# Attention scores in float32, two heads side by side on TensorE's rows, with one PSUM bank for h

## The chip, the cores and the metric

The kernel runs on one core of one Trainium2 chip. The metric is the time of the core in microseconds (us). The core has five engines with queues of their own: TensorE (PE; its weight loads are listed as PEld), VectorE (DVE), ScalarE (ACT), GpSimd (POOL), and SyncE (SP), which issues DMAs. PSUM has eight banks that hold the products until another engine reads them.

## The reference

Windowed attention over 8 batches, 8 heads, 576 positions of 64 features, then a two-layer network on its output. All data are float32.

```python
scores = scale * np.matmul(q, k.transpose(0, 1, 3, 2))
slopes = 2.0 ** (-8.0 * (np.arange(H, dtype=np.float32) + 1) / H)
mask = (rel >= 0) & (rel < 128)                    # rel = query - key
scores = np.where(mask, scores + slopes * -np.abs(rel), -1e9)
attn = softmax(scores); x = attn @ v               # x: 4608 x 512
h = x @ w_in                                       # 512 -> 2048
g = h * erf(softplus(h))
out = g @ w_out                                    # 2048 -> 512
```

## The kernel before

Heads go in pairs: 32 pairs (8 batches of 4), each with a q and a k array of 128 rows, 64 rows for each of the two heads. A pair has five tiles of 128 queries (`QTILES`, the last overlaps the fourth): tile 0 sees 128 keys, tiles 1 to 3 see 256, tile 4 sees 192. Tiles 0 to 2 are span 0, tiles 3 and 4 span 1. The first eight pairs run span 0 of all eight, then span 1; later pairs run whole.

One tile's way: scores on TensorE into PSUM (line 511, or 497 for the first spans), bias and row minimum on VectorE (522), exponential on ScalarE (532), sums on VectorE (549, 550), scaling on GpSimd (560), transposes on TensorE (578, tile `t`), copies out of PSUM (472 on ScalarE, 474 on VectorE), products with v on TensorE (596, `px`).

The scores are taken in one of two ways. Spans of the first four pairs (`EARLY`) use two float32 products, one for each head, on 64 rows each, in two PSUM buffers; q alone is scaled, by VectorE (line 435). All others split q and k for the float32r type: `kh` is k in float32r (451 on VectorE or 453 on ScalarE), `kl` what is left of it (463, VectorE), and `a` holds q in float32r on one half of the rows (472 or 474) and its residual on the other (466, GpSimd). Then four products of 128 rows fill one bank for both heads. For that k is loaded twice, once for each half of the rows, through one raw buffer each for k and q.

The second part (`Moe`) runs in units: a chunk of 384 tokens by 128 hidden features. A unit takes 12 products into `h` (line 782, PSUM, two buffers), a copy to SBUF (766 on ScalarE or 768 on VectorE), softplus and erf on ScalarE (811, 813), products on VectorE (824, 829), and 9 products into `o` (844). 72 units use the first 6 blocks of the weights and 120 the other 10. Weights are prepared by VectorE, ScalarE and GpSimd (lines 670 to 692), `x` is split by VectorE (759).

The order of all work is fixed when the program is built. `Plan.run` takes every operation with an assumed cost, a due time `at` and its buffers, and places it on its engine when its inputs and buffers are free, the earliest due first. Forty warm-up products (line 383) fill TensorE where nothing else is ready. So other costs or other buffers give another order on every engine.

PSUM's eight banks before: `h` two, `o` three, `s`, `t` and `x` one each.

Of the kernel before, what the change touches and what calls it, by code (L numbers as in the profile page):

```python
# [19 lines left out]
P = 128  # L20
# [13 lines left out]
EARLY = 4  # L34
# [6 lines left out]
PB, XB, OB, TB, TBB = 8, 3, 3, 2, 2  # L41
BT = 0
# [279 lines left out]
def step_time(n):  # L322
    return TE * min(n, NE) + TA * max(0, n - NE)
# [19 lines left out]
class Attention:  # L343


    def __init__(self, tc, plan, ctx, actx, qT, kT, vb, bias, ident, moe):
# [5 lines left out]
        self.raw, self.split, self.pp, self.ptp, self.xsb = (  # L352
            sb(n) for n in ("raw", "split", "pp", "ptp", "xsb")
        )
# [10 lines left out]
        self.seq = 0  # L365
# [20 lines left out]
    def operands(self, i, w=None):  # L386

        nc, op = self.nc, self.plan.op
        sync = nc.sync.dma_start
        b, g = self.order[i]  # L390
        at = step_time(self.step) - LL
        q0, q1 = (0, S) if w is None else SPANS[w][1:3]
        k0 = max(0, q0 - WIN)
        nq, nk = q1 - q0, q1 - k0
        early = self.seq < EARLY
        nm = f"{i}_{w}"
        tags = [("a0", "kh0"), ("a1", "kh1"), ("kl0", "kl1")][self.seq // 2 % 3]
        self.seq += 1
        if early:
            q = Buf(self.split, [P, S], F32, tags[0], 2, "a" + nm)  # L400
            k = Buf(self.split, [P, S], F32, tags[1], 2, "k" + nm)
            op(emit=lambda e: sync(k[:, :nk], self.kT[b, g, :, k0:q1]), w=[k], at=at, **dma(P * nk * 4))
        else:
            q = Buf(self.raw, [P, S], F32, "qr", 1, "qr" + nm)
            k = Buf(self.raw, [P, 2, S], F32, "kr", 1, "kr" + nm)
            src = self.kT[b, g, :, k0:q1].rearrange("(j d) s -> d j s", j=2)

            def both(e):
                for half in range(2):
                    sync(k[half * D : (half + 1) * D, :, :nk], src)  # L410

            op(emit=both, w=[k], at=at, **dma(2 * P * nk * 4, 2, 0.65))
        op(emit=lambda e: sync(q[:, :nq], self.qT[b, g, :, q0:q1]), w=[q], at=at, **dma(P * nq * 4))
        at = step_time(self.step) - LP
        return (*(self.early_parts if early else self.parts)(nm, g, q, k, nq, nk, at), q0, k0)
# [16 lines left out]
    def early_parts(self, nm, g, q, k, nq, nk, at):  # L432
        for j in range(2):
            rows = slice(j * D, (j + 1) * D)
            self.plan.op({"DVE": dve(nq, True)}, lambda e, j=j, rows=rows: self.nc.vector.tensor_scalar(
                q[rows, :nq], q[rows, :nq], 2.0 ** (2 * g + j), None, op0=ALU.mult), r=[q], w=[q], at=at)
        return q, k, None

    def parts(self, nm, g, q, k, nq, nk, at):

        nc, op = self.nc, self.plan.op
        lo, hi = slice(0, D), slice(D, P)
        a = [Buf(self.split, [P, S], F32R, f"a{j}", 2, f"a{nm}_{j}") for j in range(2)]
        kh = [Buf(self.split, [P, S], F32R, f"kh{j}", 2, f"kh{nm}_{j}") for j in range(2)]
        kl = [Buf(self.split, [P, S], F32R, f"kl{j}", 2, f"kl{nm}_{j}") for j in range(2)]

        def scaled(e, out, src, by):
            if e == "DVE":  # L450
                nc.vector.tensor_scalar(out, src, by, None, op0=ALU.mult)
            else:
                nc.scalar.mul(out, src, by)

        either = lambda n: {"DVE": dve(n, True), "Act": act(n)}
        for j in range(2):
            own, other = (lo, hi) if j == 0 else (hi, lo)
            by = 2.0 ** (2 * g + j)
            op(either(nk), lambda e, j=j, by=by: scaled(e, kh[j][:, :nk], k[:, j, :nk], by),
               r=[k], w=[kh[j]], at=at)  # L460
            op(either(nq), lambda e, j=j, own=own: self.copy(e, a[j][own, :nq], q[own, :nq]),
               r=[q], w=[a[j]], at=at)
            op({"DVE": dve(nk)}, lambda e, j=j, by=by: nc.vector.scalar_tensor_tensor(
                kl[j][:, :nk], k[:, j, :nk], by, kh[j][:, :nk], op0=ALU.mult, op1=SUB),
                r=[k, kh[j]], w=[kl[j]], at=at)
            op({"Pool": pool_tt(nq)}, lambda e, j=j, own=own, other=other: nc.gpsimd.tensor_tensor(  # L466
                a[j][other, :nq], q[own, :nq], a[j][own, :nq], SUB), r=[q, a[j]], w=[a[j]], at=at)
        return a, kh, kl

# [6 lines left out]
    def scores(self, i, t, operands, low, total, at):  # L476
# [5 lines left out]
        a, kh, kl, q0, k0 = operands  # L482
        k0 = start - WIN + c0 * 64 - k0
        q0 = start - q0
        src = []
        if kl is None:

            ways = [((self.ps, "s", 1), (self.ps, "t", 1))]
            if i < NPAIR and t < 3:
                ways = [((self.ps, "s", 1), (self.spare[1], "o0", 1)), ((self.spare[0], "h", 2),) * 2]  # L490
            for j, (pool, tag, bufs) in enumerate(ways[self.step % len(ways)]):
                src.append((Buf(pool, [P, 2, 256], F32, tag, bufs, f"s{i}_{t}_{j}"), 0))

            def products(e):
# [473 lines left out]
```

## Time and profile before

| what | value |
|---|---|
| median of 3 runs | 1118.45 us (1116.33 to 1119.25) |
| profiled execution | 1118.25 us |
| its span, first to last instruction | 1116.3 us |
| TensorE busy | 1073.7 us (96%) |
| ScalarE busy | 721.9 us (65%) |
| VectorE busy | 684.9 us (61%) |
| GpSimd busy | 385.7 us (35%) |
| mean granted TensorE clock | 0.983 of 2.4 GHz |

A matmul's time in the profile runs until its result is out, and the next one starts long before that; what a matmul keeps TensorE for is read from start to start. A float32 product stands as two matmuls. Names are the program's, with buffer numbers left out: `s` scores, `p` probabilities, `t` transposes, `st` row minima and sums. "<-" behind an idle time names what ended it.

### The profile page before, as it was taken

How to read it: one execution, taken by the hardware profiler on the slowest of the kernel's cores; microseconds unless marked ns; L12 is line 12 of the kernel's file. 1: busy time of each engine (PE TensorE's matmuls, PEld its weight loads, DVE VectorE, ACT ScalarE, POOL GpSimd, SP SyncE). 2: the span in 40 equal slices, each digit the busy share in tenths (PEclk: the TensorE clock that was granted, in tenths of full speed). 3: DMA queues.
4: the chain of work that ended last, by engine and by line, in shares of the span. 5: the costliest groups of instructions: out<-in, count | busy, mean ns of one | idle time of the engine just before them, and what ended most of it. 6: DMA issues, size and time to landing. Idle time of an engine off the chain costs nothing.

```text
span 1116.3 us, 17069 instructions
## 1 busy us (share of the span) xinstructions
PE 1073.7 (96%) x6000; PEld 976.5 (87%) x6000; DVE 684.9 (61%) x1602; ACT 721.9 (65%) x1436; POOL 385.7 (35%) x464
## 2 busy tenths in 40 slices
PE   9776979999999999999999999999999999999998
PEld 8666968988899999999899998899999999999996
DVE  5878898887888888775867675333433433433332
ACT  6567667878788787776677675355455455455462
POOL 5776887646666566653333231000000000000000
PEclk9797999999999999999999999999999999999999
DMA  6444555444545455422343422202202202202102
GB/s 184 139 132 122 140 152 153 146 132 115 163 118 135 121 143 149 118 89 78 114 132 114 141 69 74 86 13 73 85 19 67 85 19 67 85 13 73 57 19 67
DMA packets 89732, 111.59 MB, mean 100 GB/s; under 512 B 45744, under 2 KB 59696, under 8 KB 89648
## 3 DMA queue, kind: packets, MB, share of 16 engines
q1 hardware_dynamic: 89648, 110.52, 33.5%
q8 instruction: 47, 0.77, 0.3%
q14 instruction: 37, 0.30, 0.1%
HBM read 82.18 MB, written 28.31 MB: 99 GB/s over the span
## 4 chain that ended last, share of the span: by engine, by line
PE 82%; DVE 9%; POOL 3%; DMA 2%; issue 2%; ACT 2%; POOLq 0%; SPq 0%; DVEq 0%; ACTq 0%
PE o L844 32%; PE h L782 31%; PE px L596 7%; PE s L511 5%; PE t L578 5%; POOL p L560 2%; DMA xr<-xd 2%; DVE p L522 1%; PE warm_ps L383 1%; DVE xl L759 1%; POOL wto L686 1%; DVE hs L824 1%; DVE gl L829 1%; PE s L497 1%; ACT p L532 1%
## 5 line engine op out<-in xcount | busy, mean ns | idle before, releaser
L782 PE MATMUL h<-xh,whi 128*128 128x384 f32 x768 | 262.5, 342 | 0.0
L782 PE MATMUL h<-xl,whi 128*128 128x384 f32 x768 | 259.2, 338 | 1.6 <-DVE xl L759 1.6
L782 PE MATMUL h<-xh,wli 128*128 128x384 f32 x768 | 259.7, 338 | 0.0
L560 POOL TENSOR_SCALAR p<-p,st 128x256 f32<-128x256 f32 (+2 forms) x320 | 194.0, 623 | 128.1 <-DVE st L550 108.1
L844 PE MATMUL o<-who,gh 128*128 128x512 f32 x576 | 228.8, 397 | 0.6 <-DVE ot L768 0.6
L844 PE MATMUL o<-who,gl 128*128 128x512 f32 x576 | 227.6, 395 | 1.2 <-DVE gl L829 1.2
L844 PE MATMUL o<-wlo,gh 128*128 128x512 f32 x576 | 227.3, 395 | 1.2 <-POOL wlo L692 0.7
L766 ACT COPY hs<-h 128x384 f32<-128x384 f32 x137 | 65.3, 477 | 215.1 <-PE h L782 214.6
L532 ACT ACTIVATE p<-p,st 128x256 f32<-128x256 f32 (+2 forms) x320 | 149.0, 468 | 24.5 <-DVE st L522 23.6
L782 PEld LDWEIGHTS h<-xl,whi 128*128 128x128 f32 x768 | 145.2, 189 | 8.7 <-DVE xl L759 2.1
L782 PEld LDWEIGHTS h<-xh,whi 128*128 128x128 f32 x768 | 145.3, 189 | 6.9 <-ACT hs L766 0.2
L782 PEld LDWEIGHTS h<-xh,wli 128*128 128x128 f32 x768 | 144.8, 189 | 0.2 <-POOL wli L692 0.2
L844 PEld LDWEIGHTS o<-who,gl 128*128 128x128 f32 x576 | 108.1, 188 | 25.4 <-DVE gl L829 2.1
L522 DVE CUSTOM_DVE_ANT_0 p<-s,bias_sb 128x256 f32<-128x256 f32 (+2 forms) x320 | 109.4, 378 | 33.4 <-PE s L511 21.6
L768 DVE COPY hs<-h 128x384 f32<-128x384 f32 x55 | 30.4, 554 | 160.8 <-PE h L782 160.8
L844 PEld LDWEIGHTS o<-wlo,gh 128*128 128x128 f32 x576 | 108.5, 188 | 17.9 <-POOL wlo L692 2.2
L844 PEld LDWEIGHTS o<-who,gh 128*128 128x128 f32 x576 | 108.6, 188 | 16.6 <-DVE ot L768 1.5
L824 DVE TENSOR_TENSOR hs<-s,hs 128x768 f32<-128x768 f32 x96 | 95.2, 1016 | 23.4 <-ACT s L813 23.4
L829 DVE TENSOR_TENSOR gl<-hs,gh 128x768 fp32r<-128x768 f32 x96 | 94.6, 989 | 15.5 <-ACT gh L766 14.7
L578 PE MATMUL t<-ident,p 128*128 128x128 f32 x544 | 85.7, 284 | 17.6 <-POOL p L560 11.8
L578 PEld LDWEIGHTS t<-ident,p 128*128 128x128 f32 x544 | 65.6, 147 | 30.4 <-POOL p L560 14.6
L466 POOL TENSOR_TENSOR a_None<-qr_None,a_None 64x576 fp32r<-64x576 f32 x48 | 76.4, 1592 | 25.7 <-DVE a_None L474 20.7
(80 smaller groups left out, 1653.1 us busy)
## 6 DMA issues: line engine op xcount, KB each, us to landing
xr<-xd SPq DMA_DIRECT2D x22, 768.0 KB, 4.3
kr_None<-k_t SPq DMA_DIRECT2D x48, 288.0 KB, 4.2
pd<-ot SPq DMA_DIRECT2D x36, 256.0 KB, 3.7
ot<-pd SPq DMA_DIRECT2D x36, 256.0 KB, 3.0
wri<-w_in SPq DMA_DIRECT2D x16, 512.0 KB, 3.8
wro<-w_out SPq DMA_DIRECT2D x16, 512.0 KB, 3.7
out_dram<-ot SPq DMA_DIRECT2D x32, 256.0 KB, 2.1
qr_None<-q_t SPq DMA_DIRECT2D x24, 288.0 KB, 3.1
```

Source lines behind the costliest of these rows:

```text
L466: op({"Pool": pool_tt(nq)}, lambda e, j=j, own=own, other=other: nc.gpsimd.tensor_tensor(a[j][other, :nq], q[own, :nq], a[j][own, :nq], SU ...
L511: nc.tensor.matmul(ps[:m, j, :n], lhsT=a[j][:, q0 : q0 + m], rhs=rhs[:, k0 : k0 + n], start=(o == 0), stop=(o == 1),)
L522: nc.vector.tensor_tensor_reduce(out=pt[:m, c0:c1, j, :], in0=blocks(src[j][0][:m, src[j][1], :n]), in1=blocks(self.bias[:m, c0 * 64 : c1 ...
L532: nc.scalar.activation(dst, dst, AF.Exp, bias=low[:m, j : j + 1], scale=-1.0, accum_out=total[:m, j : j + 1],)
L560: nc.gpsimd.tensor_scalar(dst, dst, totals[t][:m, j : j + 1], 1.0, op0=ALU.mult, op1=ALU.mult)
L578: nc.tensor.matmul(ps[:, col : col + P], lhsT=p[t][:, kb].rearrange("p j d -> p (j d)"), rhs=self.ident[:, :], is_transpose=True, start=no ...
L596: self.nc.tensor.matmul(dst[:, q0 - base : q1 - base], lhsT=v[:, blk], rhs=sb[sbi][:, off : off + q1 - q0], start=(blk == order[0][0]), st ...
L766: self.nc.scalar.copy(out, src)
L782: nc.tensor.matmul(ps[:, :CH], lhsT=ww[:, cs], rhs=xx[:, k], start=(k2 + k + n == 0), stop=(k2 + k + n == 4),)
L824: V if e == "DVE" else G).tensor_tensor(hs[:, :n], s[:, :n], hs[:, :n], ALU.mult),
L829: V if e == "DVE" else G).tensor_tensor(gl[:, :n], hs[:, :n], gh[:, :n], SUB),
L844: nc.tensor.matmul(po.all, lhsT=g[:, j, cs], rhs=w.all, start=(u["start"] and n == 0), stop=(u["end"] and n == 2),)
```

## The change

All tiles take the early way. q and k of a pair are loaded once, in three buffers each, and never split. One VectorE instruction for each load scales q by 4^g and by 1 or 2 for the two heads, from a column that GpSimd sets at the start. Each tile's scores are two float32 products on 64 rows each, in two buffers of `s`, one bank each; the first spans also use one buffer of `h` and one of `o` in turn. `h` has one bank instead of two. The planner's cost of a score group on TensorE becomes 2 x max(n / 1200, 0.205) + 0.15 us.

```diff
--- before.py
+++ after.py
-EARLY = 4
+QB = 3
...
+        self.heads = Buf(sb("heads"), [P, 1], F32, "heads", 1, "heads")
+        for j in range(2):
+            plan.op({"Pool": 0.2}, lambda e, j=j: self.nc.gpsimd.memset(
+                self.heads[j * D : (j + 1) * D], 2.0**j), w=[self.heads], at=-1)
...
-        early = self.seq < EARLY
         nm = f"{i}_{w}"
-        tags = [("a0", "kh0"), ("a1", "kh1"), ("kl0", "kl1")][self.seq // 2 % 3]
-        self.seq += 1
-        if early:
-            q = Buf(self.split, [P, S], F32, tags[0], 2, "a" + nm)
-            k = Buf(self.split, [P, S], F32, tags[1], 2, "k" + nm)
-            op(emit=lambda e: sync(k[:, :nk], self.kT[b, g, :, k0:q1]), w=[k], at=at, **dma(P * nk * 4))
-        else:
-            q = Buf(self.raw, [P, S], F32, "qr", 1, "qr" + nm)
-            k = Buf(self.raw, [P, 2, S], F32, "kr", 1, "kr" + nm)
-            src = self.kT[b, g, :, k0:q1].rearrange("(j d) s -> d j s", j=2)
-            def both(e):
-                for half in range(2):
-                    sync(k[half * D : (half + 1) * D, :, :nk], src)
-            op(emit=both, w=[k], at=at, **dma(2 * P * nk * 4, 2, 0.65))
+        q = Buf(self.split, [P, S], F32, "q", QB, "q" + nm)
+        k = Buf(self.split, [P, S], F32, "k", QB, "k" + nm)
+        op(emit=lambda e: sync(k[:, :nk], self.kT[b, g, :, k0:q1]), w=[k], at=at, **dma(P * nk * 4))
         op(emit=lambda e: sync(q[:, :nq], self.qT[b, g, :, q0:q1]), w=[q], at=at, **dma(P * nq * 4))
-        at = step_time(self.step) - LP
-        return (*(self.early_parts if early else self.parts)(nm, g, q, k, nq, nk, at), q0, k0)
+        op({"DVE": dve(nq, True)}, lambda e: nc.vector.tensor_scalar(
+            q[:, :nq], q[:, :nq], self.heads[:, 0:1], 4.0**g, op0=ALU.mult, op1=ALU.mult),
+           r=[q, self.heads], w=[q], at=step_time(self.step) - LP)
+        return q, k, q0, k0
...
-    def early_parts(self, nm, g, q, k, nq, nk, at):
-        for j in range(2):
-            rows = slice(j * D, (j + 1) * D)
-            self.plan.op({"DVE": dve(nq, True)}, lambda e, j=j, rows=rows: self.nc.vector.tensor_scalar(
-                q[rows, :nq], q[rows, :nq], 2.0 ** (2 * g + j), None, op0=ALU.mult), r=[q], w=[q], at=at)
-        return q, k, None
-    def parts(self, nm, g, q, k, nq, nk, at):
-        nc, op = self.nc, self.plan.op
-        lo, hi = slice(0, D), slice(D, P)
-        a = [Buf(self.split, [P, S], F32R, f"a{j}", 2, f"a{nm}_{j}") for j in range(2)]
-        kh = [Buf(self.split, [P, S], F32R, f"kh{j}", 2, f"kh{nm}_{j}") for j in range(2)]
-        kl = [Buf(self.split, [P, S], F32R, f"kl{j}", 2, f"kl{nm}_{j}") for j in range(2)]
-        def scaled(e, out, src, by):
-            if e == "DVE":
-                nc.vector.tensor_scalar(out, src, by, None, op0=ALU.mult)
-            else:
-                nc.scalar.mul(out, src, by)
-        either = lambda n: {"DVE": dve(n, True), "Act": act(n)}
-        for j in range(2):
-            own, other = (lo, hi) if j == 0 else (hi, lo)
-            by = 2.0 ** (2 * g + j)
-            op(either(nk), lambda e, j=j, by=by: scaled(e, kh[j][:, :nk], k[:, j, :nk], by),
-               r=[k], w=[kh[j]], at=at)
-            op(either(nq), lambda e, j=j, own=own: self.copy(e, a[j][own, :nq], q[own, :nq]),
-               r=[q], w=[a[j]], at=at)
-            op({"DVE": dve(nk)}, lambda e, j=j, by=by: nc.vector.scalar_tensor_tensor(
-                kl[j][:, :nk], k[:, j, :nk], by, kh[j][:, :nk], op0=ALU.mult, op1=SUB),
-                r=[k, kh[j]], w=[kl[j]], at=at)
-            op({"Pool": pool_tt(nq)}, lambda e, j=j, own=own, other=other: nc.gpsimd.tensor_tensor(
-                a[j][other, :nq], q[own, :nq], a[j][own, :nq], SUB), r=[q, a[j]], w=[a[j]], at=at)
-        return a, kh, kl
...
-        a, kh, kl, q0, k0 = operands
+        q, k, q0, k0 = operands
         k0 = start - WIN + c0 * 64 - k0
         q0 = start - q0
-        src = []
-        if kl is None:
-            ways = [((self.ps, "s", 1), (self.ps, "t", 1))]
-            if i < NPAIR and t < 3:
-                ways = [((self.ps, "s", 1), (self.spare[1], "o0", 1)), ((self.spare[0], "h", 2),) * 2]
-            for j, (pool, tag, bufs) in enumerate(ways[self.step % len(ways)]):
-                src.append((Buf(pool, [P, 2, 256], F32, tag, bufs, f"s{i}_{t}_{j}"), 0))
-            def products(e):
-                for j in range(2):
-                    rows = slice(j * D, (j + 1) * D)
-                    nc.tensor.matmul(
-                        src[j][0][:m, src[j][1], :n], lhsT=a[rows, q0 : q0 + m],
-                        rhs=kh[rows, k0 : k0 + n], start=True, stop=True,
-                    )
-            op({"PE": 2 * fp32_us(n) + 0.05}, products, r=[a, kh], w=[src[0][0], src[1][0]],
-               at=at, rows=0.5)
-        else:
-            ps = Buf(self.ps, [P, 2, 256], F32, "s", 1, f"s{i}_{t}")
-            src = [(ps, 0), (ps, 1)]
-            def products(e):
-                for j in range(2):
-                    for o, rhs in enumerate((kh[j], kl[j])):
-                        nc.tensor.matmul(
-                            ps[:m, j, :n], lhsT=a[j][:, q0 : q0 + m], rhs=rhs[:, k0 : k0 + n],
-                            start=(o == 0), stop=(o == 1),
-                        )
-            op({"PE": 4 * f32r_us(n) + 0.05}, products, r=[*a, *kh, *kl], w=[ps], at=at)
+        ways = [((self.ps, "s", 2),) * 2]
+        if i < NPAIR and t < 3:
+            ways.append(((self.spare[0], "h", 1), (self.spare[1], "o0", 1)))
+        src = [
+            (Buf(pool, [P, 512], F32, tag, bufs, f"s{i}_{t}_{j}"), 0)
+            for j, (pool, tag, bufs) in enumerate(ways[self.step % len(ways)])
+        ]
+        def products(e):
+            for j in range(2):
+                rows = slice(j * D, (j + 1) * D)
+                nc.tensor.matmul(
+                    src[j][0][:m, :n], lhsT=q[rows, q0 : q0 + m], rhs=k[rows, k0 : k0 + n],
+                    start=True, stop=True,
+                )
+        op({"PE": 2 * max(n / 1200.0, 0.205) + 0.15}, products, r=[q, k], w=[x[0] for x in src],
+           at=at, rows=0.8)
         pt = Buf(self.pp, [P, 4, 2, 64], F32, "p", PB, f"p{i}_{t}")
         blocks = lambda x: x.rearrange("p (c d) -> p c d", d=64)
         def biased(e):
             for j in range(2):
                 nc.vector.tensor_tensor_reduce(
-                    out=pt[:m, c0:c1, j, :], in0=blocks(src[j][0][:m, src[j][1], :n]),
+                    out=pt[:m, c0:c1, j, :], in0=blocks(src[j][0][:m, :n]),
                     in1=blocks(self.bias[:m, c0 * 64 : c1 * 64]),
...
-        ps = Buf(self.ps_h, [P, 512], F32, "h", 2, f"h{U}")
+        ps = Buf(self.ps_h, [P, 512], F32, "h", 1, f"h{U}")
```

The planner's order changes on every engine. TensorE's queue in the middle of attention, before: transposes `t`, one tile's scores `s_2`, then the second half of a unit's `h`.

```order
L578 MATMUL t_0_0_4353<-ident,p_1_4185 128x128 x2
L578 MATMUL t_0_0_4353<-ident,p_2_4213 128x128 x2
L511 MATMUL s_2_4361<-kh_None_4097,a_None_4102 128x256
L511 MATMUL s_2_4361<-kl_None_4120,a_None_4102 128x256
L511 MATMUL s_2_4361<-kh_None_4109,a_None_4147 128x256
L511 MATMUL s_2_4361<-kl_None_4155,a_None_4147 128x256
L782 MATMUL h_4338<-xh_1_3887,whi_1263 128x384
L782 MATMUL h_4338<-xl_1_3908,whi_1263 128x384
L782 MATMUL h_4338<-xh_1_3887,wli_1266 128x384
```

The same engine, the same kind of place, now:

```order
L518 MATMUL t_1_1_3723<-ident,p_4_3638 128x128
L518 MATMUL t_1_1_3723<-ident,p_3_3602 128x128
L450 MATMUL s_2_0_3726<-k_None,q_None 128x256
L450 MATMUL s_2_1_3728<-k_None,q_None 128x256
L536 MATMUL px_1_3733<-pb_3710,vbd_158 128x192
L536 MATMUL px_1_3733<-pb_3710,vbd_158 128x64
L536 MATMUL px_1_3733<-pb_3710,vbd_158 128x128 x2
```

Four products over the full rows, which read split k and q, have become two that read k and q as loaded.

GpSimd's queue early in attention, before: probabilities `p` of the fourth and fifth pair, the residual of q (`a`), and the first sum for a block of weights (`wti`).

```order
L560 TENSOR_SCALAR p_1_396<-p_1_396,st_0_369 128x4x64 x2
L560 TENSOR_SCALAR p_2_428<-p_2_428,st_0_369 128x4x64 x2
L466 TENSOR_TENSOR a_0_0_484<-qr_0_433,a_0_0_484 64x384
L466 TENSOR_TENSOR a_0_1_502<-qr_0_433,a_0_1_502 64x384
L560 TENSOR_SCALAR p_0_454<-p_0_454,st_0_455 128x2x64 x2
L560 TENSOR_SCALAR p_1_520<-p_1_520,st_0_455 128x4x64 x2
L560 TENSOR_SCALAR p_2_542<-p_2_542,st_0_455 128x4x64 x2
L466 TENSOR_TENSOR a_0_0_596<-qr_0_563,a_0_0_596 64x384
L466 TENSOR_TENSOR a_0_1_605<-qr_0_563,a_0_1_605 64x384
L686 TENSOR_TENSOR wti_555<-wti_555,wqi_508 128x512
```

And now:

```order
L500 TENSOR_SCALAR p_1_421<-p_1_421,st_0_377 128x4x64 x2
L500 TENSOR_SCALAR p_2_435<-p_2_435,st_0_377 128x4x64 x2
L626 TENSOR_TENSOR wti_339<-wti_339,wqi_296 128x512
L500 TENSOR_SCALAR p_0_451<-p_0_451,st_0_452 128x2x64 x2
L500 TENSOR_SCALAR p_1_487<-p_1_487,st_0_452 128x4x64 x2
L500 TENSOR_SCALAR p_2_508<-p_2_508,st_0_452 128x4x64 x2
L632 TENSOR_TENSOR wli_599<-wti_339,whi_563 128x512
```

The rows of `a` are gone, and the weights' first sum and its residual `wli` have moved up by a pair or more.

TensorE's queue where attention has ended, before: the end of one unit's `h` products and the start of the next unit's.

```order
L782 MATMUL h_7211<-xh_1_7136,whi_6551 128x384
L782 MATMUL h_7211<-xl_1_7145,whi_6551 128x384
L782 MATMUL h_7211<-xh_1_7136,wli_6572 128x384
L782 MATMUL h_7230<-xh_0_6987,whi_6610 128x384
L782 MATMUL h_7230<-xl_0_6995,whi_6610 128x384
L782 MATMUL h_7230<-xh_0_6987,wli_6620 128x384
```

And now:

```order
L722 MATMUL h_7010<-xh_1_6839,whi_6109 128x384
L722 MATMUL h_7010<-xl_1_6841,whi_6109 128x384
L722 MATMUL h_7010<-xh_1_6839,wli_6120 128x384
L722 MATMUL h_7029<-xh_0_6556,whi_6185 128x384
L722 MATMUL h_7029<-xl_0_6565,whi_6185 128x384
L722 MATMUL h_7029<-xh_0_6556,wli_6192 128x384
```

In both the units follow without other work between them. Before, there are thirteen such places behind attention's end, and the two units write two banks; now there are five, and both units write the one bank.

## Rows read from the trace of the kernel before

**Rows 1.** Busy time by stage; columns: stretch, length, PE, PEld, DVE, ACT, POOL, clock, DMA.
```profile
0.00:130.00 130.00, 106.68 (x638) 96.79 (x639) 99.87 (x318) 86.60 (x244) 91.36 (x123) 0.87 0.52 145
130.00:510.00 380.00, 367.00 (x2352) 338.32 (x2351) 310.67 (x915) 298.81 (x762) 235.39 (x296) 1.00 0.47 131
510.00:1116.30 606.30, 600.00 (x3014) 541.42 (x3012) 274.34 (x370) 336.53 (x432) 58.92 (x47) 1.00 0.22 71
```

**Rows 2.** Longest waits in stage A; columns: us in total, times, longest us.
```profile
POOL p L560 <- DVE st L550: 16.6, 6, 9.1
...
PE s L511 <- DVE st L522: 10.2, 8, 2.0
...
PE t L578 <- POOL p L560: 7.8, 3, 5.4
```

**Rows 3.** Chain of waits in stage A, in order of time: start us, us, what.
```profile
33.39 2.49 DMA qr<-q_t
```

**Rows 4.** Timeline of TensorE: first product of a score group and the matmul behind it.
```profile
380.29 0.28 PE L511 MATMUL s<-kh_None,a_None 128*128 128x256 f32 x1
...
380.76 0.40 PE L844 MATMUL o<-who,gh 128*128 128x512 f32 x1
...
384.40 0.36 PE L511 MATMUL s<-kh_None,a_None 128*128 128x256 f32 x1
...
384.95 0.98 PE L596 MATMUL px<-pa,vbd 128*128 128x192 f32 x6
...
403.05 0.25 PE L511 MATMUL s<-kh_None,a_None 128*128 128x192 f32 x1
...
403.47 0.36 PE L782 MATMUL h<-xh,whi 128*128 128x384 f32 x1
...
405.58 0.22 PE L511 MATMUL s<-kh_None,a_None 128*128 128x128 f32 x1
...
405.97 0.45 PE L844 MATMUL o<-who,gh 128*128 128x512 f32 x1
```

**Rows 5.** Timeline of TensorE, early tiles: groups of four and warm-up matmuls.
```profile
7.41 0.70 PE L497 MATMUL s<-k,a 64*128 64x256 f32 x4
8.04 1.38 PE L383 MATMUL warm_ps<-warm 128*128 128x128 f32 x10
9.35 0.49 PE L497 MATMUL s<-k,a 64*128 64x128 f32 x4
9.77 0.71 PE L383 MATMUL warm_ps<-warm 128*128 128x128 f32 x4
10.41 1.13 PE L497 MATMUL s<-k,a 64*128 64x256 f32 x8
11.48 1.83 PE L383 MATMUL warm_ps<-warm 128*128 128x128 f32 x14
```

**Rows 6.** Busy time in stage A of lines 463, 451 and 466, one after the other.
```profile
0.00:130.00 130.00, 14.30 (x26) 0.87 0.52 145
...
0.00:130.00 130.00, 6.93 (x15) 0.87 0.52 145
...
0.00:130.00 130.00, 25.92 (x26) 0.87 0.52 145
```

**Rows 7.** Chain of waits in stage C.
```profile
563.73 2.10 PE h L782 x12
565.83 2.08 PE o L844 x9
```

**Rows 8.** Timeline: a unit's last h product, and its copy.
```profile
655.47 0.33 PE L782 MATMUL h<-xh,wli 128*128 128x384 f32 x1
...
655.84 0.48 ACT L766 COPY hs<-h 128x384 f32<-128x384 f32 x1 [1.60 <-PE h L782]
```

**Rows 9.** Timeline: the same of a unit in stage B.
```profile
205.18 0.33 PE L782 MATMUL h<-xh,wli 128*128 128x384 f32 x1
...
222.36 0.48 ACT L766 COPY hs<-h 128x384 f32<-128x384 f32 x1
```

More of the change, by code (lines that the diff above doesn't have):

```diff
@@ L351, in __init__ @@
         ps = lambda name: ctx.enter_context(tc.tile_pool(name=name, bufs=1, space=PSUM))
-        self.raw, self.split, self.pp, self.ptp, self.xsb = (
-            sb(n) for n in ("raw", "split", "pp", "ptp", "xsb")
-        )
+        self.split, self.pp, self.ptp, self.xsb = (sb(n) for n in ("split", "pp", "ptp", "xsb"))
         self.ps = ps("ps_a")
@@ L364, in __init__ @@
         self.step = self.loads = 0
-        self.seq = 0
+        self.heads = Buf(sb("heads"), [P, 1], F32, "heads", 1, "heads")
+        for j in range(2):
+            plan.op({"Pool": 0.2}, lambda e, j=j: self.nc.gpsimd.memset(
+                self.heads[j * D : (j + 1) * D], 2.0**j), w=[self.heads], at=-1)
         self.warm_up()
@@ L481, in scores @@
         n = (c1 - c0) * 64
-        a, kh, kl, q0, k0 = operands
+        q, k, q0, k0 = operands
         k0 = start - WIN + c0 * 64 - k0
         q0 = start - q0
-        src = []
-        if kl is None:
-            ways = [((self.ps, "s", 1), (self.ps, "t", 1))]
-            if i < NPAIR and t < 3:
-                ways = [((self.ps, "s", 1), (self.spare[1], "o0", 1)), ((self.spare[0], "h", 2),) * 2]
-            for j, (pool, tag, bufs) in enumerate(ways[self.step % len(ways)]):
-                src.append((Buf(pool, [P, 2, 256], F32, tag, bufs, f"s{i}_{t}_{j}"), 0))
-            def products(e):
-                for j in range(2):
-                    rows = slice(j * D, (j + 1) * D)
-                    nc.tensor.matmul(
-                        src[j][0][:m, src[j][1], :n], lhsT=a[rows, q0 : q0 + m],
-                        rhs=kh[rows, k0 : k0 + n], start=True, stop=True,
-                    )
-            op({"PE": 2 * fp32_us(n) + 0.05}, products, r=[a, kh], w=[src[0][0], src[1][0]],
-               at=at, rows=0.5)
-        else:
-            ps = Buf(self.ps, [P, 2, 256], F32, "s", 1, f"s{i}_{t}")
-            src = [(ps, 0), (ps, 1)]
-            def products(e):
-                for j in range(2):
-                    for o, rhs in enumerate((kh[j], kl[j])):
-                        nc.tensor.matmul(
-                            ps[:m, j, :n], lhsT=a[j][:, q0 : q0 + m], rhs=rhs[:, k0 : k0 + n],
-                            start=(o == 0), stop=(o == 1),
-                        )
-            op({"PE": 4 * f32r_us(n) + 0.05}, products, r=[*a, *kh, *kl], w=[ps], at=at)
```

## The prediction

> **What bounds the kernel now.** I read the page first: TensorE is busy 96% of the span, so no other engine can be the bound on average. Then I cut the span by what stands in TensorE's queue: stage A (0 to 130 us, attention with the first units of the second part and most of their weights), stage B (130 to 510, attention and units mixed), stage C (510 to the end, units alone). The row for each stage [rows 1] says what an average hides. In C TensorE has 600.0 us of work in 606.3: nothing can be gained there, only lost. In B it idles 13.0 us of 380 at full clock. In A it is busy 106.7 of 130 us at a mean granted clock of 0.87, VectorE 99.9, GpSimd 91.4, ScalarE 86.6: no engine is full, they pass work round. The list of waits in A [rows 2] names the ring: TensorE waits for VectorE (a score bank is read out) 10.2 us and for GpSimd (probabilities are scaled) 7.8 us; GpSimd waits for VectorE 16.6 us. The chain of waits also holds a DMA for q of 2.49 us [rows 3], since q has one raw buffer. So the change is worth what it takes off this ring in A, less what it adds to TensorE in B.
>
> **TensorE's scores.** Before, all but the first twelve tiles (of 128 queries) use four float32r products. Start to start, to the next matmul, they hold TensorE 0.47 us at 256 keys (380.29 to 380.76), 0.55 us after a px product (384.40 to 384.95), 0.42 at 192 and 0.39 at 128 [rows 4]. I take 0.50, 0.42, 0.39. After, each tile is what the first twelve already are: two float32 products on 64 rows each, which stand in the trace as four matmuls. From such a group's start to the next matmul is 0.63 us at 256 keys (7.41 to 8.04) and 0.42 at 128 (9.35 to 9.77) [rows 5]. That isn't all. Ten warm-up matmuls between two such groups take 1.31 us (8.04 to 9.35), four take 0.64 (9.77 to 10.41): 0.112 each, and 0.19 us left over each time, for leaving one group and entering the next. A lone group thus costs 0.63 + 0.19 = 0.82 us at 256 keys, 0.61 at 128, and by the middle of the two 0.715 at 192. Two groups in a row (10.41 to 11.48) take 1.07, so the heads do run at once, and the left-over is paid per switch; in the new queue nearly every group stands alone.
>
> The trace's 0.63 us start to start is half again what two heads side by side need if nothing but their columns counted. The Trainium skill, "TensorE: Matmul & The Clock Gate", Part 3 (packing small matmuls), says that matmuls on different row groups cost one matmul's time and some 4 ns for each further one; "TensorEngine Tiling (Array Packing)", Tiling Modes, says that a change of tiling mode drains TensorE. By the first alone a group would cost 0.43 us and the sum would come out near 1076; by the second with the left-over of the rows it is the 0.82 above. The rows bear out the second between float32 matmuls; none shows a switch beside the long float32r ones.
>
> Stage B holds 24 pairs of heads of five tiles, three of 256 keys, one of 192, one of 128. Each pair grows by 3 x 0.32 + 0.295 + 0.22 = 1.475 us, so B's queue on TensorE grows by 35 us. Against this stand the waits in B: 13.0 us idle [rows 1], at most 26 with what each restart costs behind it (I allow as much again). VectorE, ScalarE and GpSimd lose all split work there, so waits shrink; the work left over is near all TensorE's. I take 13 us back. B: +35 - 13 = +22 us, bounds +9 and +35.
>
> **Stage A.** The residual kl (line 463) costs VectorE 14.3 us, the residual of q (line 466) costs GpSimd 25.9 us [rows 6]; kh (line 451) costs VectorE 6.9 us, 0.46 each. Up to the fortieth tile's bias pass its queue loses also 14 casts and 8 scalings; at the same 0.46 (an estimate) that is 31 us in all. It gains 19 scalings of q, 9 us, and in the new order some fifteen copies and steps of weights that stood on ScalarE or later, at 0.48 to 1.0 each (estimate: the copy of rows 8 and twice that) some 11 us: a net loss of about 10 us. GpSimd's is all of the 25.9, since nothing takes its place but weights moved up. If VectorE alone set A's end, A would shorten by 10; if the ring shortened with GpSimd's and VectorE's work and the wait for q (now three buffers, and k comes once, not twice) went too, by 30. TensorE's own 8 us more (28 changed tiles at 1.475 / 5) lie beside these waits. With no engine full, the middle: -20 us. What is late next in A is VectorE's bias pass and the weights' steps on it.
>
> **h's single bank.** In C, h (2.10 us) and o (2.08) alternate [rows 7], so the copy of h's bank has o's 2.08 us, and in C's bulk nothing changes. But the new order puts h directly behind h at five places where C begins (before: thirteen, with two banks). There TensorE must wait for the copy: the last matmul of a unit starts at 655.47, the copy runs from 655.84 for 0.48 us [rows 8]; less the 0.17 us a matmul is followed after, plus a hop back of 0.1 (estimate from the same gap), that is 0.8 us each, +4 us. If the copy is behind other work, twice; if work slips in between, none: 0 to 8.
>
> **Sum.** The profiled execution took 1118.25 us, 1.95 outside its span of 1116.3; it stands 0.2 below the median, 1118.45. A -20, B +22, C +4: +6, so **1124 us**. The new memset of the scaling column on GpSimd and the k loads, one in place of two on SP, I cost at nothing: both lie ahead of the first score or beside A's ring. At the bounds' ends: -30 + 9 + 0 gives 1097, -10 + 35 + 8 gives 1151.
>
> **Rivals.**
> - *The ring was the real cost.* A loses 30, B gives back 26 of its 35, C nothing much (+4): 1118 - 30 + 9 + 4 = 1101. For it: half the waits of A end at the very engines that are relieved. Against it: in B only 13 us are idle by the rows, and the bias pass stays on VectorE. It decides from the point where A and B together give back more than the 39 us that B and C add.
> - *h's bank stalls B too.* In the kernel before a copy may lag far: the last h matmul of a unit starts at 205.18, its copy on ScalarE at 222.36 [rows 9]. With one bank the next unit must wait for that, and the new order has 55 units ahead of attention's end. If half of them cost 0.8 us more, that is +22 on the forecast: 1146. Against it: the new order puts other matmuls between units nearly everywhere in B.
> - *Row groups nearly free.* A switch beside float32r work costs nothing: B falls by 24 x 0.56 = 13 us rather than growing by 35. 1118 - 20 - 13 - 13 + 4 = 1076. Against it: the 0.63 and 0.19 of rows 5.
>
> **Chances.** Forecast 0.57 (own range 1114 to 1134), ring 0.25, bank 0.13, free groups 0.05. What a measurement tells from no change is about 0.3%, 3.4 us: 1115 to 1122. The ring and the free groups are faster (0.30, and 0.01 of the forecast's low end); a third of the forecast's own range lies within, with little from the ring 0.17; the rest, 0.52, is slower. For 8 in 10 I leave out the free groups and the ends of the ring and the bank: 1104 to 1142.
>
> **What would show it.** Right: a lone score group of 256 keys near 0.8 us of TensorE in B, A some 20 us shorter at its fortieth tile, B longer by about 22 with TensorE idle under 10 us, five gaps of 0.8 us where C begins, C's bulk as before. Wrong: groups near 0.5 us; a front that shrinks by over 30 us; gaps in front of h throughout B; or a granted clock that falls in B, which stands at 1.00 now.

## The result, and the profile after

The changed kernel took 1126.7 us (median of 4 runs, 1125.51 to 1128.53) against 1118.04 us for the kernel before in the same comparison: a ratio of 1.008, with a 95% interval of 1.006 to 1.010. It is 0.8% slower; 1124 had been forecast. (Of one experiment, the full-row products, two executions of twelve took 2213.5 us, with TensorE's steps over twice as long from end to end; its median is of the other ten, and its profile is of a repeat.)

First the three stages of the changed kernel, with the columns of [rows 1]: stretch, length, busy time of PE, PEld, DVE, ACT, POOL, clock, DMA.

```profile
0.00:130.00 130.00, 117.60 (x691) 95.50 (x692) 95.08 (x322) 78.00 (x227) 69.32 (x108) 0.92 0.49 142
130.00:510.00 380.00, 378.53 (x2263) 303.93 (x2262) 223.96 (x799) 252.80 (x682) 135.52 (x239) 1.00 0.35 107
510.00:1126.60 616.60, 607.88 (x3050) 546.61 (x3048) 283.52 (x385) 343.18 (x442) 61.19 (x48) 1.00 0.21 70
```

Against [rows 1], GpSimd lost 91 - 69 = 22 us of work in A and 100 in B, VectorE 87 in B. TensorE now idles 1.5 us in B, where it idled 13.0: everything round it has become lighter, and TensorE has become fuller. The list of waits in A, which answers to [rows 2]:

```profile
POOL p L500 <- DVE st L490: 39.9, 12, 9.1
ACT p L472 <- DVE st L462: 15.0, 13, 4.3
DVE p L462 <- PE s L450: 9.1, 11, 2.4
DVE q L402 <- DMA q<-q_t: 8.7, 7, 3.7
...
PEld s L450 <- DVE st L462: 7.1, 7, 2.6
```

TensorE's own wait for scores to be read (10.2 us in [rows 2]) has fallen to 4.7 and is off the top of the list; GpSimd waits more (39.9 us for 16.6), which costs nothing by itself. A new row is VectorE's wait for the load of q. Whether it matters only the chain of waits says (start us, us, what):

```profile
22.67 0.63 PE s L450 x4
23.30 1.24 PE t L518 x10
24.54 0.68 PE s L450 x4
...
25.24 0.33 SPq L399
...
25.63 3.08 DMA q<-q_t
...
28.73 0.42 DVE q L402
```

```profile
33.49 0.84 PE s L450 x4
34.34 0.33 SPq L399
...
34.72 4.23 DMA q<-q_t
...
38.97 0.49 DVE q L402
```

In both pieces the chain goes from the end of a score group to a load on SP (line 399 is the load of k, the one of q is behind it); the load takes 3 or 4 us, and VectorE scales q. A third one stands at 111.95 for 4.63 us, behind `px` products. A load's buffer is one of three, and the scores of the load three places back must have read it. For the first of the three that was the wait: the group that frees the buffer ends at 25.18, the load goes out at 25.24. The chain draws the second in the same way, but there the group that frees the buffer had ended at 32.86 (the one on the chain is the next), and SP issued loads of v and a store first:

```profile
32.26 1.27 SPq L416 DMA_DIRECT2D vbd<-v_b  x2
33.63 0.56 SPq L582 DMA_DIRECT2D xd<-xr  x1
34.28 0.38 SPq L399 DMA_DIRECT2D k<-k_t  x1
```

The third is of this kind too: its buffer is free at 108.61, and SP comes to it at 110.05. Where a load stands in SP's queue the planner sets, by the buffers it counts. Before, two such loads stood on A's chain: the one of 2.49 us in [rows 3], and a second one that [rows 3] doesn't show:

```profile
91.01 2.42 DMA qr<-q_t
```

So 4.9 us in two loads have become 11.9 in three.

A lone score group in attention, which answers to [rows 4] (timeline of TensorE):

```profile
395.31 0.39 PE L784 MATMUL o<-wlo,gh 128*128 128x512 f32 x1
395.54 0.40 PE L784 MATMUL o<-who,gl 128*128 128x512 f32 x1
395.86 0.59 PE L450 MATMUL s<-k_None,q_None 64*128 64x192 f32 x4
396.39 0.50 PE L784 MATMUL o<-who,gh 128*128 128x512 f32 x1
396.73 0.39 PE L784 MATMUL o<-wlo,gh 128*128 128x512 f32 x1
```

`o` products follow each other at 0.23 us. Ahead of the group the step is 0.32 (0.09 too long), the group itself takes 0.53, and the first `o` behind it 0.34 (0.11 too long): 0.73 us in all. Over all lone groups at full clock the median is 0.832, 0.725 and 0.62 us at 256, 192 and 128 keys (0.82, 0.715 and 0.61 forecast), beside float32r work just as beside float32 work. The same count for the split groups of before gives 0.478, 0.45 and 0.448, in the mean 0.505, 0.471 and 0.451; the means of after are 0.835, 0.723 and 0.627, so a tile grew by 0.284 us in the mean over a pair's five.

Where attention has ended, one bank makes TensorE wait (timeline of TensorE and of ScalarE; it answers to [rows 8]):

```profile
658.34 0.33 PE L722 MATMUL h<-xl,whi 128*128 128x384 f32 x1
658.51 0.34 PE L722 MATMUL h<-xh,wli 128*128 128x384 f32 x1
659.42 0.44 PE L722 MATMUL h<-xh,whi 128*128 128x384 f32 x1 [0.57 <-ACT hs L706]
659.70 0.33 PE L722 MATMUL h<-xl,whi 128*128 128x384 f32 x1
```

```profile
658.89 0.48 ACT L706 COPY hs<-h 128x384 f32<-128x384 f32 x1 [2.93 <-PE h L722]
```

There are five such gaps of 0.57 us, beginning at 658.85, 661.80, 673.12, 676.07 and 683.20. From start to start, 658.51 to 659.42 is 0.91 us in place of 0.17, and the next step is 0.28: 0.84 us each. A sixth wait for this bank in C, of 0.40 us, ends at 612.40, behind `o` products; one of 0.80 us stands in A, ending at 118.31.

To compare stages although units move between them, I take from the time at which a stage ends what TensorE had by then spent on units: 0.175 us for each `h` product and 0.231 for each `o` (2.10 / 12 and 2.08 / 9 of [rows 7]). The rest is the stage's own time. The 40th tile ends A (its bias pass on VectorE), the last px product ends B. Before, the 40th bias pass (the second of its two instructions) starts at 131.7 us with 114 `h` and 9 `o` products done: 131.7 - 19.9 - 2.1 = 109.7. By this count, for the kernels below too (with the prices rounded as here the entries come out within 0.3 us of these):

| kernel | A | B | C | sum | median us |
|---|---|---|---|---|---|
| before | 109.7 | 196.2 | 8.3 | 314.2 | 1118.0 |
| changed | 99.6 | 212.7 | 12.2 | 324.5 | 1126.7 |
| changed, six buffers | 91.0 | 214.0 | 12.2 | 317.2 | 1121.1 |
| the same, real costs in the planner | 92.3 | 214.6 | 12.2 | 319.1 | 1122.5 |
| split scores, one bank for h, one for s | 109.9 | 205.1 | 14.4 | 329.4 | 1133.7 |
| split scores, one bank for h, two for s | 113.0 | 195.2 | 11.0 | 319.2 | 1121.9 |
| groups for 40 tiles, then split | 100.0 | 189.0 | 12.3 | 301.3 | 1102.1 |
| groups for 80 tiles, then split | 91.9 | 200.8 | 12.1 | 304.8 | 1107.1 |
| full rows, six buffers | 90.5 | 213.6 | 7.2 | 311.3 | 1115.0 |

The change is A -10.1, B +16.5, C +3.9: +10.3 us, which is the whole difference of the two spans (1116.3 and 1126.6). Each row is read from one execution, and executions of one kernel lie up to 7 us apart (1119.6 to 1126.5 with the real costs): two or three microseconds between two rows show nothing by themselves.

### The profile page after: what moved, and what is told of

It is laid out like the page before. It is cut to its first block, busy times and chain, and to the rows that moved or that the text cites. A ratio compares the mean times of both kernels' runs of the same rounds, so it can differ in the third digit from the quotient of the medians.

```text
span 1126.6 us, 16542 instructions
## 1 busy us (share of the span) xinstructions
PE 1104.0 (98%) x6000; PEld 946.0 (84%) x6000; DVE 602.6 (53%) x1504; ACT 674.0 (60%) x1350; POOL 266.0 (24%) x394
## 4 chain that ended last, share of the span: by engine, by line
PE 92%; DVE 3%; DMA 2%; POOL 1%; ACT 1%; issue 0%; SPq 0%; POOLq 0%; DVEq 0%; ACTq 0%
PE h L722 35%; PE o L784 35%; PE px L536 8%; PE s L450 8%; PE t L518 6%; PE warm_ps L384 1%; DMA q<-q_t 1%; POOL p L500 1%; DMA xr<-xd 1%; DVE hs L764 1%; DVE wto L613 0%; DMA q_None<-q_t 0%; DMA pd<-ot 0%; DVE xl L699 0%; DVE xh L708 0%
## 5 line engine op out<-in xcount | busy, mean ns | idle before, releaser
L722 PE MATMUL h<-xh,whi 128*128 128x384 f32 x768 | 267.6, 348 | 4.1 <-ACT hs L706 3.3
L500 POOL TENSOR_SCALAR p<-p,st 128x256 f32<-128x256 f32 (+2 forms) x320 | 176.3, 569 | 289.4 <-DVE st L490 209.6
L784 PE MATMUL o<-who,gh 128*128 128x512 f32 x576 | 232.9, 404 | 0.9 <-DVE ot L804 0.9
L472 ACT ACTIVATE p<-p,st 128x256 f32<-128x256 f32 (+2 forms) x320 | 149.4, 470 | 39.9 <-DVE st L462 39.6
L462 DVE CUSTOM_DVE_ANT_0 p<-s,bias_sb 128x256 f32<-128x256 f32 (+2 forms) x320 | 109.7, 380 | 89.8 <-PE s L450 84.7
L784 PEld LDWEIGHTS o<-who,gh 128*128 128x128 f32 x576 | 108.2, 188 | 30.9 <-issue 12.3
L784 PEld LDWEIGHTS o<-who,gl 128*128 128x128 f32 x576 | 108.0, 188 | 23.5 <-DVE gl L769 0.2
L764 DVE TENSOR_TENSOR hs<-s,hs 128x768 f32<-128x768 f32 x96 | 92.0, 980 | 26.0 <-ACT s L753 26.0
L450 PE MATMUL s<-k_None,q_None 64*128 64x256 f32 (+2 forms) x480 | 76.7, 396 | 0.0
```

The source lines that it names most:

```text
L450: nc.tensor.matmul(src[j][0][:m, :n], lhsT=q[rows, q0 : q0 + m], rhs=k[rows, k0 : k0 + n], start=True, stop=True,)
L462: nc.vector.tensor_tensor_reduce(out=pt[:m, c0:c1, j, :], in0=blocks(src[j][0][:m, :n]), in1=blocks(self.bias[:m, c0 * 64 : c1 * 64]), sca ...
L472: nc.scalar.activation(dst, dst, AF.Exp, bias=low[:m, j : j + 1], scale=-1.0, accum_out=total[:m, j : j + 1],)
L500: nc.gpsimd.tensor_scalar(dst, dst, totals[t][:m, j : j + 1], 1.0, op0=ALU.mult, op1=ALU.mult)
L722: nc.tensor.matmul(ps[:, :CH], lhsT=ww[:, cs], rhs=xx[:, k], start=(k2 + k + n == 0), stop=(k2 + k + n == 4),)
L764: V if e == "DVE" else G).tensor_tensor(hs[:, :n], s[:, :n], hs[:, :n], ALU.mult),
```

## The experiments

Each median below stands beside one of the kernel before from the same set of runs, 1117.0 to 1117.6 us. The kernels are told in the order of the questions.

**Are three buffers too few?** The changed kernel, with

```diff
-QB = 3
+QB = 6
```

> The changed kernel with six buffers each for q and k in place of three, so that a load need not wait until a pair three places earlier has been scored. Theory (front A fell short of the forecast because the q loads, on the chain at 25.63, 34.72 and 111.95 us for 3.08, 4.23 and 4.63 us, wait for score groups): the DMA steps leave the chain, the 40th tile comes 4 to 8 us earlier than the changed kernel's 116.5 us, total about 1120 us. Rival (VectorE's bias pass and weight steps set the front, the loads only stand beside them): 40th tile at 115 to 118 us, total 1126 to 1128 us.

1121.1 us, ratio to before 1.0032 (1.0018 to 1.0047). The eighth load goes out at 11.76 us instead of 34.28, the chain to 118 us holds no load of q any more (two stores of x, of 4.59 and 5.34 us, now stand on it), and the 40th bias pass starts at 107.7 us instead of 121.6. That is more than the 4 to 8 us expected, but fewer unit products are done by then: 8.6 us of A's own time go, while C stays as it was and B is within 1.3 us. Its first stages:

```profile
0.00:130.00 130.00, 119.33 (x736) 95.82 (x736) 94.61 (x332) 88.44 (x251) 75.28 (x112) 0.96 0.58 174
130.00:510.00 380.00, 378.62 (x2256) 305.13 (x2257) 229.63 (x807) 254.63 (x675) 132.64 (x238) 1.00 0.32 97
```

The list of waits in A of the same kernel alone would have misled:

```profile
DVE q L402 <- DMA q<-q_t: 9.0, 7, 3.6
```

VectorE waits for q as long as with three buffers (8.7), but none of it stands on the chain. That three buffers are too few holds, by the chain and by the time; that each load waits for scores does not.

**What does h's one bank cost without row groups?** The kernel before, split scores, with

```diff
-ways = [..., ((self.spare[0], "h", 2),) * 2]
+ways = [..., ((self.spare[0], "h", 1), (self.ps, "u", 1))]
...
-        ps = Buf(self.ps_h, [P, 512], F32, "h", 2, f"h{U}")
+        ps = Buf(self.ps_h, [P, 512], F32, "h", 1, f"h{U}")
```

> The kernel before, split scores as they were, with one PSUM bank for h in place of two (the first tiles' scores, which used both banks of h, use the one and a bank of their own). Theory (one bank costs only where units stand back to back after attention): some 4 us, 1122 us, a gap of 0.57 us at each place where h follows h, in the 130 to 510 us stretch no more idle time than the 13.0 us of before. Rival (the copy of h lags in the stretch with attention too, 3.35 us on average before): 15 us or more, 1133 us and over, with gaps in front of h throughout attention.

1133.7 us, 1.0141 (1.0121 to 1.0161): here the rival's time is right, not my theory's. C pays 6.1 us and B 8.9. The rival's "gaps in front of h throughout attention" don't show, though. From the 40th pass to the last px product TensorE idles 18.9 us, where it idled 12.0, and waits for this bank in three places (us in total, times, longest us):

```profile
PE h L782 <- ACT hs L766: 5.1, 3, 3.5
```

The granted clock is at its lower level for 10.2 us of B, for 3.4 before. The longest of the three places, on the engines in order of time:

```profile
144.31 0.95 DVE L824 TENSOR_TENSOR hs<-s,hs 128x768 f32<-128x768 f32 x1
145.28 0.83 ACT L766 CAST gh<-hs 128x768 fp32r<-128x768 f32 x1 [2.56 <-DVE hs L824]
146.02 0.47 ACT L766 COPY hs<-h 128x384 f32<-128x384 f32 x1
...
146.55 0.69 PE L782 MATMUL h<-xh,whi 128*128 128x384 f32 x1 [3.47 <-ACT hs L766]
```

ScalarE has the copy of `h` behind a cast of `gh`, the cast waits 2.56 us for VectorE, and so TensorE waits 3.47 us for the bank. This is the lag of [rows 9], now with somebody waiting for it.

**And with the change's second bank for s?** The same with two buffers of `s` for the split scores, so that its banks are those of the changed kernel:

```diff
-            ps = Buf(self.ps, [P, 2, 256], F32, "s", 1, f"s{i}_{t}")
+            ps = Buf(self.ps, [P, 2, 256], F32, "s", 2, f"s{i}_{t}")
```

> The kernel before with its split scores, but with the banks of the changed kernel: one for h, two for s. It holds the banks fixed, so that it and the six-buffer kernel (1121.1 us) differ by the scores and their operands alone. Theory (TensorE's growth in attention, +22 us from the 40th tile to the last px product, comes from the row groups): 40th tile near 131 us as before, from there to the last px product 390 to 400 us, a second buffer of s taking back part of what one bank of h costs (1133.7 us with one s): 1120 to 1130 us. Rival (that growth is h's one bank): 40th tile to last px 408 us or more, 1135 us or more.

1121.9 us, 1.0043 (1.0028 to 1.0058), within the theory's 1120 to 1130. The 40th bias pass starts at 127.9, where 131 had been expected. B's own time is 195.2, as before; the second bank of `s` gives back the 8.9 us and one more, although the copy of `h` still lags behind the unit's end, by 2.4 us in the mean. At equal banks the scores are then told apart: this kernel against six buffers has A 113.0 against 91.0, B 195.2 against 214.0, and the same total within a microsecond. The growth of B belongs to the float32 scores (those over full rows, below, grow it as much), not to h's bank. By tiles: against this kernel six buffers are 23.1 us ahead at the 80th tile, 14.0 at the 120th and 4.6 at the 160th, so each tile from the 80th on loses 0.23 us.

**Groups in front, split behind.** The kernel just told, with

```diff
-EARLY = 4
+EARLY = 16
```

> The same kernel, with row groups and one load of k for the first eight pairs (40 tiles) and split scores for the other 24 pairs. Theory (row groups gain 24 us in the front with deep buffers and lose 22 us behind it): 40th tile at 106 to 115 us, from there to the last px product as with split scores throughout, total 15 to 24 us below that kernel, near 1105 us. Rival (the front's gain is work put off, which is paid behind it): 40th tile as early, but the rest longer by as much, total within 5 us of the kernel with split scores throughout.

1102.1 us, 0.986 (0.984 to 0.989): faster than both kernels by 15 and 25 us. The total came as the theory has it, 20 us below the kernel with split scores throughout. The place didn't: the 40th bias pass starts at 124.0, not at 106 to 115, and only 13.0 us of the gain stand in A, 6.2 in B. Its first two stages:

```profile
0.00:130.00 130.00, 114.98 (x686) 94.47 (x687) 101.54 (x331) 84.68 (x240) 77.92 (x110) 0.93 0.50 142
130.00:510.00 380.00, 372.92 (x2404) 346.39 (x2403) 298.65 (x895) 298.69 (x758) 227.10 (x295) 1.00 0.46 132
```

The first splits for the later pairs fall ahead of the 40th bias pass here: 11.1 us of work in all, 4.65 of them GpSimd's residuals of q. A is 9.0 us longer than with six buffers; that these splits are the reason is likely, not shown.

**How far should the groups go?**

```diff
-EARLY = 16
+EARLY = 24
```

> As the kernel with row groups for the first eight pairs (1102.1 us), but for the first sixteen pairs (80 tiles), split scores for the other sixteen. Theory (row groups gain while other engines hold TensorE, which in the traces so far lasts to about the 80th tile, and lose 0.22 us a tile from there on): 1097 to 1103 us. Rival (the gain ends with the front's 40 tiles, and the next 40 lose 0.3 us each): 1110 to 1116 us.

1107.1 us, 0.990 (0.988 to 0.992): between the two expectations, 5 us behind the kernel with 40 tiles. A, which now holds no splits, is 8.1 us shorter; B is 11.8 longer. So the next 40 tiles neither gain nor lose 0.3 us each; in all they lose about 0.1. The chain of this kernel to 115 us holds four loads of q, 12.2 us together, and its A is still within a microsecond of that with six buffers: that a load stands on the chain doesn't say what it costs.

**What in a group costs 0.83 us?** The kernel with six buffers, each pair of products issued twice (the second pair writes the same values again):

```diff
-                for j in range(2):
+                for j in (0, 1, 0, 1):
```

> The six-buffer kernel with each tile's two 64-row products issued twice, one pair directly behind the other, into the same banks (the second writes the same values); all else in the same order. It prices what a group costs when TensorE is already in this shape. Theory (of a lone group's 0.83 us at 256 keys only about 0.43 is its columns, the rest is paid once for going in and out): a second group adds 0.44, 0.33, 0.22 us at 256, 192, 128 keys, 60 us over 160 tiles, less what stands beside waits in the front: 1170 to 1182 us. Rival (0.83 us is what the columns themselves take on 64 rows): 3.84 us more per pair, 123 us, 1230 to 1245 us.

1176.6 us, 1.0517 (1.0484 to 1.0551): 55 us more than with single pairs, not 123. Timeline of TensorE, a doubled group in front of `o`:

```profile
391.70 1.13 PE L450 MATMUL s<-k_None,q_None 64*128 64x256 f32 x8
392.76 0.50 PE L784 MATMUL o<-who,gh 128*128 128x512 f32 x1
393.10 0.40 PE L784 MATMUL o<-wlo,gh 128*128 128x512 f32 x1
```

And a single one in the changed kernel:

```profile
393.64 0.70 PE L450 MATMUL s<-k_None,q_None 64*128 64x256 f32 x4
394.27 0.50 PE L784 MATMUL o<-who,gh 128*128 128x512 f32 x1
394.61 0.40 PE L784 MATMUL o<-wlo,gh 128*128 128x512 f32 x1
```

1.06 us against 0.63, with the same 0.34 behind both. Over all groups the second pair adds 0.431, 0.325 and 0.226 us at 256, 192 and 128 keys. A lone group's 0.832, 0.725 and 0.624 is that and 0.40 each time: what a group costs beyond its columns doesn't depend on its size here and is paid once for a run of groups, for going in and out. Over 160 tiles it is 64 us.

The Trainium skill, "TensorEngine Tiling (Array Packing)", Tiling Modes, says that changing the tiling mode drains TensorE; the 0.40 us paid once a group, and not for a second pair, agrees. The page gives no price.

**The same scores without 64-row groups.** Six buffers, with q laid out twice, each copy zero but for one head's rows (`z`), two products over all 128 rows into one bank, and two banks for `h`:

```diff
-                    src[j][0][:m, :n], lhsT=q[rows, q0 : q0 + m], rhs=k[rows, k0 : k0 + n],
+                    ps[:m, j, :n], lhsT=q[:, j, q0 : q0 + m], rhs=k[:, k0 : k0 + n],
...
-        ps = Buf(self.ps_h, [P, 512], F32, "h", 1, f"h{U}")
+        ps = Buf(self.ps_h, [P, 512], F32, "h", 2, f"h{U}")
```

> The six-buffer kernel with q laid out twice, each copy zero but for one head's rows, so that a tile's scores are two float32 products on all 128 rows, one after the other, into one bank; so h keeps two banks. Theory (leaving and entering the 64-row groups costs as much as it saves): a lone tile of 256 keys holds TensorE near 0.87 us against 0.83, one of 128 keys 0.45 against 0.62, per pair 3.70 against 3.84; from the 40th tile to the last px product 3 us shorter, behind it 4 us shorter for h's second bank, VectorE 9 us more in the front: 1115 to 1122 us. Rival (the heads at once save what they promise): a tile of 256 keys at 0.87 us against 0.45 in the groups when nothing is left over, 10 us or more slower than the six-buffer kernel, 1131 us or more.

> The kernel with zero-padded q and full-row products once more, for a profile at the usual clock: a lone tile of 256 keys holds TensorE near 0.87 us and one of 128 near 0.45, the time within 3 us of 1116 us, no gaps before h where attention has ended. If a switch of shape cost nothing, the tile would still be 0.87 us but the kernel slower than the six-buffer kernel by 10 us, which its time already speaks against.

1115.3 us, 0.998 (0.996 to 0.999), and in the repeat 1115.0, 0.998 (0.996 to 1.000): 6 us below six buffers, about 0.2% below the kernel before. A tile holds TensorE for 0.865, 0.653 and 0.448 us, which sum to 3.70 us a pair as expected, though each product streams on its own. Timeline of TensorE:

```profile
387.17 0.39 PE L783 MATMUL o<-wlo,gh 128*128 128x512 f32 x1
387.39 0.42 PE L783 MATMUL o<-who,gl 128*128 128x512 f32 x1
387.65 1.03 PE L450 MATMUL s<-k_None,z_None 128*128 128x256 f32 x4
388.33 0.58 PE L783 MATMUL o<-who,gh 128*128 128x512 f32 x1
388.75 0.39 PE L783 MATMUL o<-wlo,gh 128*128 128x512 f32 x1
```

Two heads at once save nothing over two heads in turn while each tile's group stands alone. No gap stands before `h` where attention has ended, and C's own time is 7.2: the second bank of `h` is worth 5.0 us there. In B, where 3 us had been expected from the scores, 0.4 show (213.6 against 214.0); what the second bank alone does there these runs don't tell.

**Does the planner's wrong cost matter?** Six buffers, with the groups' measured time as their cost:

```diff
-        op({"PE": 2 * max(n / 1200.0, 0.205) + 0.15}, products, ...
+        op({"PE": 0.41 + n / 600.0}, products, ...
```

> The six-buffer kernel with the planner's cost of a score group set to what the trace of the changed kernel shows, 0.41 + n / 600 us (0.84, 0.73, 0.62 for 256, 192, 128 keys) in place of 0.58, 0.56, 0.56. Only the order of work changes. Theory (the order hides waits well enough, the loss is the groups' own time): within 4 us of 1121 us. Rival (the order made with too low a cost is itself part of the loss): 1117 us or less.

1122.5 us, 1.0048 (1.0032 to 1.0063) against 1.0032 (1.0018 to 1.0047) without: no difference that these runs show. That the order is what is lost, the rival, would have been 1117 us or less.

**Row groups with two banks for h.** Two kernels keep the banks of before. There a tile behind the first spans has only the banks of `s` and `t` for its two heads:

```diff
-EARLY = 4
+EARLY = 16
```

> The kernel before with row groups for the spans of the first eight pairs (its first 40 tiles) in place of the first four spans; later pairs split, h keeps two banks. Theory (front gains what the split's work costs there, the later stage loses 0.32 us for each tile on row groups): 40th tile near 117 us in place of 129.4, from there as before: about 1105 us. Rival (the front's gain in the changed kernel came from work moved out of the front and is paid back behind it): 1115 to 1119 us.

and for all tiles:

```diff
-EARLY = 4
+EARLY = 40
```

> The kernel before with row groups for all tiles, h with two banks; behind the first spans a tile's two banks are then the one of s and the one of t. Theory (the loss is TensorE's 0.83 us for a group against 0.48, wherever it has work; h's single bank costs only 4 us): about as the changed kernel less 4 us, plus what the shared bank of t costs: 1122 to 1135 us, gaps before h at the end of attention gone. Rival (the single bank of h is the larger part of the loss): 1112 us or less.

1185.3 us, 1.0595 (1.0573 to 1.0617), and 1478.3 us, 1.321 (1.319 to 1.324). All four expectations fail, and the kernels don't answer the question they were made for: I had taken the shared bank for a small cost. The longest waits of the second:

```profile
POOL p L560 <- DVE st L550: 428.9, 50, 18.9
DVE p L522 <- PE s L497: 323.0, 122, 10.1
...
POOL p L560 <- ACT p L532: 180.4, 20, 13.2
PEld t L578 <- POOL p L560: 158.7, 79, 6.6
PE t L578 <- POOL p L560: 128.6, 79, 6.3
```

VectorE waits for scores, GpSimd for VectorE, the transposes for GpSimd, and the next scores for the bank of the transposes, since they share it: a tile at a time, 5.5 us each (202.2 us at the 40th bias pass, 421.9 at the 80th). The first has the same groups for the same 40 tiles as the kernel of 1102.1 us; the banks alone (and one bank of `h` for two) make 83 us.

The Trainium skill, "TensorEngine Tiling (Array Packing)", Gotcha 1: PSUM Pressure, warns that row tiles write to different banks and raise the demand for them; the 83 us are what that was worth here.

## Why the prediction was right, and where it was not

The forecast of slower came true, and B and C moved by the mechanism given. That 1124 stands so near 1126.7 is in part luck, since two errors partly cancel: A gained 10 less than forecast, B lost 5.5 less.

- **A, -20 forecast, -10.1 measured.** The step that failed is "the wait for q (now three buffers, and k comes once, not twice) went too". It did not: on the chain two loads with 4.9 us became three with 11.9. I had counted the buffers and not asked when a load goes out: the first waits for a score group that must free its buffer, the other two stand late in SP's queue. With six the term measures -18.7. That -10 is also the prediction's number for VectorE alone setting A's end is chance: the further 8.6 us came from buffers of q and k and nothing else. By account: 28 changed tiles add 8.0 us; TensorE's idle time up to the 40th bias pass falls from 24.3 to 12.4 (9.7 with six buffers); and its clock rises. The granted clock in A is 0.87 in [rows 1], 0.92 after and 0.96 with six buffers, which over 130 us makes 34, 21 and 10 us at 1.2 in place of 2.4 GHz. At half a microsecond lost for each (an estimate, and the most it can be), the clock gives back 7 and 12. The sums, -11 and -19, are near what was measured. My working had no term for the clock.
- **B, +22 forecast, +16.5 measured.** The price of a lone group was within 0.02 us, also beside float32r work, where the rows of before showed none. The growth is 24 x 1.418 = 34 us by the means (35 forecast), the idle time falls by 10.5 us, from 12.0 (13 forecast). That makes +23.5; about 1.7 are given back by the clock, low for 3.4 us in B before and not at all after. The 5 us still missing I can't place. Nor is B even: from the 40th to the 80th tile the waits given back, 7.8 us, and the clock take up most of the growth of 11.3 (own time -1.3 us); the loss of 17.7 us comes in the last 80 tiles, 0.22 us each, where only 3 us of waits were left to give back.
- **C, +4 forecast, +3.9 measured.** Five places, 0.84 us each, as worked out from [rows 8]; the sixth wait, of 0.40 us, was not foreseen, and the sum of all is some 0.7 us above what was measured.
- **h's bank in B.** In the changed kernel the rival fails: the copy of `h` starts 0.6 us behind the unit's end in the mean (3.3 before), and no wait for it shows in TensorE's idle time there. ScalarE and VectorE are the lighter by the splits (46 and 87 us in B), which I take to be why the copy is no longer queued; no run shows it. With split scores and one buffer of `s` the rival's cost holds, 8.9 us in B, in a few places. I had argued against it with the "other matmuls between units". That held with two buffers of `s`, where the copy lags by 2.4 us and B loses nothing, and not with one, where it lags by 1.8: the lag alone doesn't decide. What the second buffer of `s` changes is open.
- **The ring as the real cost, and free groups.** The first needed 30 us in A; even six buffers reach 18.7. The second needed groups near 0.45 us; they take 0.83. (Its 0.56 us a pair has no working in the prediction; by the prediction's own 0.43 a group it would be 0.48, which changes the total by 2 us.)

Taken apart by medians: the banks cost about 5 us (split scores, same banks), row groups with one load of k at those banks nothing (-0.8), and three buffers for six 5 to 6.

## What to carry to other kernels

Two small products on separate rows run at once, but entering and leaving that shape cost 0.40 us here, about what running at once saved at 256 keys and more than it saved at 128: pad to full rows, or put several groups side by side (the second pair of products here cost its columns alone; groups of different tiles side by side were not run). A change that relieves the helpers and loads the engine in the middle belongs where the helpers are late: the first 40 tiles, not all 160. Before counting a wait as gone for more buffers, ask when a load can go out: what frees its buffer, and what stands in front of it in the queue. The chain shows such a load where the list of waits doesn't, but only a run with more buffers gives its price.

## What was not expected of the hardware

The price of a switch of shape is a constant here: 0.40 us at 128, 192 and 256 keys alike. And TensorE's granted clock in A rose as its waits there fell, from 0.87 to 0.96: by the estimate above up to 12 of the 18.7 us that six buffers gain. That the waits are the cause is likely, not shown.
